# Four products of 32 tokens in place of two of 64 for the values of an mLSTM cell

## The chip, the cores and the metric

The kernel runs on one core of a Trainium2 chip. The metric is the time of one execution on the device in microseconds; several runs are made and their median is given. TensorE multiplies matrices, VectorE and ScalarE work element by element, GpSimd (POOL) does masks and small products, and SyncE (SP) issues the transfers.

## The reference

The computation has two parts. The first is an mLSTM cell over 4 batches, 8 heads, 768 tokens and a head width of 40, all in float32. Per head, with gates that are made stable by a running maximum `m`:

```
C = f * C + i * outer(v_t, k_t)        n = f * n + i * k_t
y_t = sigmoid(o_t) * (C q_t) / max(|n . q_t|, 1)
```

The second takes the cell's output as 3072 rows of 320 and computes `gelu(x @ w_in) @ w_out`, with the exact GELU and 2048 hidden columns.

## The kernel before

**Chunks.** The 768 tokens are cut into 6 chunks of 128 (numbered 0 to 5), so the recurrence becomes attention inside a chunk plus a state that is carried from chunk to chunk. For a batch `b` of a chunk, the steps of class `Cell` are:

- `weights` (ScalarE, L432): the decay matrix `W` of each head, 128 keys by 128 tokens;
- `scores` or `scores_two` (TensorE L507 or L523): keys times queries, which VectorE then multiplies into `W` (L510 or L529);
- `carry` (chunks 0 and 1: L545, L550) or `read_two` and `update_two` (later chunks: L578, L589): what the state gives to the queries, and the products of keys and weighted values that go into the state;
- `values` (L621): for each head, the weighted scores times the 128 values with a column of ones, that is 41 columns; VectorE adds what came from the state (L629);
- `finish` (L634 to L645): normalisation and output gate; `turn_y` (L656): the result is transposed into the layout of `x`; `split_x` (L674, L675).

Then `up` (L816, L827) computes the hidden columns with GELU on ScalarE (L831), and `down_steps` (L891) the second product, by sums and differences of blocks that VectorE prepares (`hidden_sums`, L748 to L750, `sum_late`, L921) and adds up (L904). The first chunk has its own steps for this (L761, L767, L868), because the weights are still being converted from their 64-bit form on VectorE and ScalarE (L357 to L374) then.

**Order.** Every engine works through its own queue in program order. That order is written out by hand as a string of letters in which each letter is a step and the digit its batch. `FRONT` plays chunks 0 and 1 and the first chunk's products; `DOWN` is played in each of the later rounds and interleaves the products `F` of one chunk with the cell of the next. Lower-case steps in `FRONT` are chunk 0, upper-case ones chunk 1; `V` is `values`. The parts of the two strings around it are:

```
FRONT: ... U U K L7 V0 K T2 r ... S2 J K W3 K V1 C2 ... J Y2 C3 X0 K V3 J K F ...
DOWN:  ... S0 K2 C0 F h0 M2 G0 G1 G2 G3 V0 V1 W2 F Q2 K3 Q3 Y0 M3 D3 F F N W3 F S2 F C2 h2 V2 V3 j F ...
```

In `DOWN`, `h0` and `h2` are `update_two` (L589), so TensorE goes from L589 straight to L621, as the letters between them are not TensorE's. In the last chunk `update_two` issues no products.

**Values in TensorE.** `Pm` holds 128 keys on the partitions and, per head, 128 tokens. A product's stationary operand is a slice `Pm[:, h, r]` of the tokens, its moving operand the head's 41 value columns, and its output goes to the partitions `r` of a PSUM tile `ph`. With `r` in `halves`, the slices have 64 tokens, and each product uses 64 of the array's 128 columns. From chunk 2 on the even heads come first, because VectorE weights them first.

Of the kernel before, what the change touches and what calls it, by code (L numbers as in the profile page):

```python
# [39 lines left out]
def kernel(  # L40
# [29 lines left out]
    R = P // 2  # L70
# [57 lines left out]
        return ob[n % NLD].rearrange("p (h d) -> p h d", d=D)  # L128

    halves = (slice(0, R), slice(R, P))  # L130

    def swapped(c, b):

        return c > 1 and b % 2 == 1
# [27 lines left out]
    def turn_of(n):  # L162

        return n % NLD if n < 2 * B else (n - 2 * B) % NQ

    def load_M(n, to=None):

        if not B <= n < NCH * B:
            return
        c, b = divmod(n, B)  # L170
        src = M_d[c - 1, b * H:(b + 1) * H, :]
        if to is not None:
            Mb[n] = to
            nc.sync.dma_start(out=to, in_=src.unsqueeze(0).to_broadcast([P, H, L]))
            return
        Mb[n] = shared([P, H, L], F32, "W") if n // 2 == NW else wts.tile([P, H, L], F32, name="W", tag="W")
        nc.sync.dma_start(out=Mb[n].rearrange("p h l -> p (h l)"),
                      in_=src.rearrange("h l -> (h l)").unsqueeze(0).to_broadcast([P, H * L]))
# [205 lines left out]
    def unread(bank):  # L384
        for _ in range(idle[0]):
            nc.tensor.matmul(bank, ident, ident, start=True, stop=True, skip_group_check=True)
        idle[0] = 0
# [4 lines left out]
    class Cell:  # L392
# [219 lines left out]
        def values(self, b):  # L612
            n = self.c * B + b
            Pm = W.pop(n)

            pool, tag = (ps_mm, "a") if self.c > 1 else (ps_h, "h")
            ph = pool.tile([P, H, D1], F32, name="ph", tag=tag)
            unread(ph.rearrange("p h d -> p (h d)")[:, 0:P])
            for h in range(H) if self.c < 2 else (*range(0, H, 2), *range(1, H, 2)):
                for r in halves:  # L620
                    nc.tensor.matmul(ph[r, h, :], Pm[:, h, r], vb[turn_of(n)][:, h, :], start=True, stop=True)  # L621
            if self.c > 1 and b > 0:
                load_M(n + NW)
            self.read(b)
            if self.c == 0:
                self.hs[b] = ph
                return
            hs = self.hs[b] = self.far.pop(b)
            nc.vector.tensor_tensor(out=hs, in0=ph, in1=hs, op=OP.add)  # L629
# [384 lines left out]
```

## Time and profile before

| | |
|---|---|
| Median of 3 runs | 480.7 us (480.67 to 480.8) |
| Span of the profiled execution, first to last instruction | 479.0 us |
| Median of the runs less that span (start and end around the instructions) | 1.7 us |
| TensorE busy | 470.5 us, 98% |
| VectorE, ScalarE, GpSimd busy | 351.5, 222.2, 70.4 us |
| Granted TensorE clock | 1.000 |
| Records of L621 | 768 matmuls, 768 weight loads |

The profiled execution's own time is the span and what lies around it; the runs' times stand within 0.13 us of each other, and 480.7 is taken for it. In the groups of instructions a line gives line, engine, operation, tiles, patch of the array in rows*columns, shape and number of records, then busy microseconds, mean nanoseconds of one record, and idle time before them with what ended it. PE is TensorE's matmul, PEld its weight load, DVE VectorE, ACT ScalarE. In a timeline or a chain a line begins with the start and the length in microseconds. Records of matmuls overlap, so the distance from start to start tells the pace and not the length of one.

### The profile page before, as it was taken

Reading aid. Unit: us, or ns where it says so; the run is one execution under the profiler, and the core shown is the slowest. Engines: PE = TensorE matmul, PEld = TensorE weight load, DVE = VectorE, ACT = ScalarE, POOL = GpSimd, SP = SyncE. Lnnn points to the kernel's source line nnn. Section 1 sums busy time; section 2 is a strip of 40 time slices with the busy share of each in tenths; the row PEclk is TensorE's granted clock in tenths of the full one; section 3 lists DMA queues with packets and bytes.
Section 4 is the critical chain, followed back from the end, with each engine's and each line's share of the span. In section 5 each row is a group of like instructions: output and inputs, shape, how many; then the busy total and the mean of one; then the engine's idle time right before and its main releaser. Section 6 shows DMA issues by size and latency. Waiting matters only on the chain.

```text
span 479.0 us, 11954 instructions
## 1 busy us (share of the span) xinstructions
PE 470.5 (98%) x4740; PEld 410.1 (86%) x4740; DVE 351.5 (73%) x762; ACT 222.2 (46%) x477; POOL 70.4 (15%) x104
## 2 busy tenths in 40 slices
PE   7899999999999999999999999999999999999997
PEld 7787888877777999977999977999977999977997
DVE  7899789798879999847589846589756599624321
ACT  6986999944532942112952113952113952112300
POOL 3001210000020225200324200324100222000000
PEclk9999999999999999999999999999999999999999
DMA  9998966289420367541356551367641350100001
GB/s 171 197 210 191 192 175 152 64 203 194 139 30 4 38 109 181 79 98 12 40 114 154 80 111 14 39 109 172 102 79 12 42 89 3 55 1 0 1 1 55
DMA packets 170423, 44.49 MB, mean 93 GB/s; under 512 B 156448, under 2 KB 163904, under 8 KB 170368
## 3 DMA queue, kind: packets, MB, share of 16 engines
q1 hardware_dynamic: 170368, 43.73, 46.4%
q8 instruction: 37, 0.61, 0.5%
q14 instruction: 18, 0.15, 0.1%
HBM read 39.58 MB, written 4.13 MB: 91 GB/s over the span
## 4 chain that ended last, share of the span: by engine, by line
PE 78%; issue 10%; DVE 7%; SPq 2%; DMA 1%; ACT 1%; POOL 0%; DVEq 0%; POOLq 0%
PE po L891 27%; PE pu L816 19%; PE po L868 7%; PE pu L761 5%; PE pu L827 5%; PE ph L621 4%; PE ps L523 2%; PE pu L767 1%; PE pf L589 1%; SPq L147 1%; PE px L656 1%; PE pf L578 1%; PE ps L507 1%; SPq L157 1%; PE pt L481 1%
## 5 line engine op out<-in xcount | busy, mean ns | idle before, releaser
L891 PE MATMUL po<-w_out,g 128*128 128x160 f32 x640 | 91.6, 301 | 0.0
L891 PEld LDWEIGHTS po<-w_out,g 128*128 128x128 f32 x640 | 87.7, 190 | 2.0 <-ACT g L831 1.8
L831 ACT ACTIVATE g<-pu 128x512 f32<-128x512 f32 x80 | 40.8, 614 | 52.9 <-PE pu L827 52.8
L891 PE MATMUL po<-w_sums,sums 128*128 128x160 f32 x320 | 47.7, 303 | 0.0
L891 PEld LDWEIGHTS po<-w_sums,sums 128*128 128x128 f32 x320 | 44.1, 190 | 0.7
L816 PE MATMUL pu<-x_hi,w_in_hi 128*128 128x512 f32 x160 | 41.7, 402 | 0.0
L666 ACT ACTIVATE x_hi<-px 128x384 fp32r<-128x384 f32 x20 | 9.8, 489 | 67.0 <-PE px L656 67.0
L816 PE MATMUL pu<-x_lo,w_in_lo 128*128 128x512 f32 x160 | 40.6, 395 | 0.0
L432 ACT ACTIVATE W<-W,aT 128x128 f32<-128x128 f32 x128 | 39.2, 388 | 0.1
L816 PEld LDWEIGHTS pu<-x_hi,w_in_hi 128*128 128x128 f32 x160 | 28.5, 188 | 9.3 <-ACT g L831 4.1
L748 DVE TENSOR_TENSOR sums<-g 128x512 f32<-128x512 f32 x20 | 13.8, 688 | 30.8 <-ACT g L831 30.8
L816 PEld LDWEIGHTS pu<-x_lo,w_in_lo 128*128 128x128 f32 x160 | 30.1, 188 | 7.2
L868 PE MATMUL po<-w_out,g 128*128 128x320 f32 x128 | 35.2, 433 | 0.0
L868 PEld LDWEIGHTS po<-w_out,g 128*128 128x128 f32 x128 | 24.0, 190 | 9.5
L831 ACT ACT_TABLE_LOAD x5 | 6.4, 1283 | 55.1 <-DMA blocks<-in_k_dram 27.6
L720 DVE TENSOR_TENSOR w_in_mid<-w_in_hi,w_in_lo 128x512 fp32r<-128x512 f32 x20 | 13.8, 688 | 24.4 <-PE pu L816 24.4
L816 PE MATMUL pu<-x_all,w_mid 128*128 128x512 f32 x80 | 31.6, 395 | 0.0
L816 PE MATMUL pu<-x_all,w_in_mid 128*128 128x512 f32 x80 | 31.6, 395 | 0.0
L444 POOL MEMSET g<- 32x1024 f32 x8 | 7.6, 945 | 150.1 <-ACT W L432 124.5
L406 POOL TENSOR_SCALAR_AFFINE_SELECT W<-W 128x1024 f32<-128x1024 f32 (+2 forms) x20 | 21.3, 1076 | 54.8 <-DMA W<-M_d 42.2
L904 DVE TENSOR_TENSOR o_sb<-po,o_sb 128x320 f32<-128x320 f32 (+1 forms) x27 | 12.5, 464 | 22.8 <-PE po L891 18.8
L761 PE MATMUL pu<-first_x,w_in 128*128 128x256 f32 x128 | 29.1, 382 | 0.1
(183 smaller groups left out, 915.6 us busy)
## 6 DMA issues: line engine op xcount, KB each, us to landing
W<-M_d SPq DMA_DIRECT2D x16, 512.0 KB, 5.6
bits<-in_moe_w_in_dram SPq DMA_DIRECT2D x20, 256.0 KB, 4.6
bits<-in_moe_w_out_dram SPq DMA_DIRECT2D x16, 320.0 KB, 3.3
ob<-in_o_gate_dram SPq DMA_DIRECT2D x24, 160.0 KB, 3.5
out_dram<-o_sb SPq DMA_DIRECT2D x24, 160.0 KB, 2.1
vb<-in_v_dram SPq DMA_DIRECT2D x14, 160.0 KB, 5.1
kb<-in_k_dram SPq DMA_DIRECT2D x14, 160.0 KB, 5.1
g<-M_d SPq DMA_DIRECT2D x4, 512.0 KB, 4.4
```

Of the source, the lines that this page charges most:

```text
L406: nc.gpsimd.affine_select(out=x, in_=x, compare_op=OP.is_ge, fill=1.0e30, base=base, pattern=[[0, H], [1, x.shape[2]]], channel_multiplier=-1)
L432: nc.scalar.activation(out=W[n][:, h, :], in_=src, func=AF.Exp, scale=-1.0, bias=aT[:, self.c, r:r + 1])
L621: nc.tensor.matmul(ph[r, h, :], Pm[:, h, r], vb[turn_of(n)][:, h, :], start=True, stop=True)
L720: nc.vector.tensor_tensor(out=w_mid[i], in0=w_hi[i], in1=w_lo[i], op=OP.add)
L748: nc.vector.tensor_tensor(out=s1, in0=a21, in1=a22, op=OP.add)
L761: nc.tensor.matmul(banks[-1][e][:, i - i0, :], in_tile(i, x)[:, e, i % 2 * P:(i % 2 + 1) * P], first_x[:, x, t0:t1], start=(x == 0 and i = ...
L816: nc.tensor.matmul(pus[i][e], w[k][:, e, i * P:(i + 1) * P], x[:, k, :], start=(n == 0 and k == 0), stop=False, skip_group_check=True)
L827: nc.tensor.matmul(pu[e], w[r, i // 2, i % 2 * P:(i % 2 + 1) * P], x[r, NX, :], start=False, stop=(n == 2), skip_group_check=True)
L831: nc.scalar.activation(out=g.t[:, HF * e + i, :], in_=pu[e], func=AF.Gelu, scale=4097.0)
L868: nc.tensor.matmul(po[b], g.t[:, f, b * L:(b + 1) * L], w_out[:, f, :], start=(f == 0), stop=(f == NF - 1))
L891: nc.tensor.matmul(bank[at][:, i, :], lhs(j, t), rhs(j), start=(first and i == 0 and j == 0), stop=(i == n - 1 and j == HF - 1), skip_grou ...
L904: nc.vector.tensor_tensor(out=to, in0=pb, in1=x, op=OP.add)
```

## The change

From the second chunk on (`self.c` of 1 and more), `values` loops over four slices of 32 tokens in place of two of 64. A head gets four products, each with a stationary operand of 128 by 32, the same 41 moving columns and an output of 32 partitions. The PSUM tile, the order of the heads and of all steps, and what is waited for stay. Chunk 0 keeps the halves.

```diff
     halves = (slice(0, R), slice(R, P))
+    quarters = tuple(slice(R // 2 * n, R // 2 * (n + 1)) for n in range(4))
...
             for h in range(H) if self.c < 2 else (*range(0, H, 2), *range(1, H, 2)):
-                for r in halves:
+                for r in halves if self.c == 0 else quarters:
                     nc.tensor.matmul(ph[r, h, :], Pm[:, h, r], vb[turn_of(n)][:, h, :], start=True, stop=True)
```

## The prediction

> **What bounds the kernel now.** I read the page first: the busy shares in 40 slices, then its chain that ended last.
>
> ```profile
> span 479.0 us, 11954 instructions
> ...
> PE   7899999999999999999999999999999999999997
> ...
> PE 78%; issue 10%; DVE 7%; SPq 2%; DMA 1%; ACT 1%; POOL 0%; DVEq 0%; POOLq 0%
> ```
>
> TensorE is busy from end to end and carries the chain, so an edit of TensorE's own stream moves the end directly, unless another engine is waiting just behind it. Second, the chain through the middle of chunk 2's cell, where each piece is TensorE:
>
> ```profile
> 162.38 1.50 PE ps L523 x64
> 163.88 0.91 PE pf L578 x64
> 164.79 2.37 PE po L891 x16
> 167.16 1.06 PE pf L589 x32
> 168.22 1.87 PE ph L621 x64
> ```
>
> L621 is the changed line. Two batches' values are 32 products; a product leaves two weight-load records and two matmul records, hence 64, in 1.87 us: 0.935 us for a batch, 29 ns a record. L578 makes the same 64 records with the same 41 moving columns in 0.91 us, 14 ns a record. Third, the groups by shape, to see why:
>
> ```profile
> L621 PE MATMUL ph<-vb,W 128*64 128x41 f32 x576 | 19.6, 231 | 0.4 <-DVE W L510 0.3
> L578 PE MATMUL pf<-state,qT 64*64 64x41 f32 x512 | 8.9, 227 | 0.0
> L621 PEld LDWEIGHTS ph<-vb,W 128*64 128x64 f32 x576 | 18.0, 138 | 1.6 <-DVE W L510 0.7 <-issue 0.5
> L891 PEld LDWEIGHTS po<-w_out,g 128*128 128x128 f32 x640 | 87.7, 190 | 2.0 <-ACT g L831 1.8
> ```
>
> The third word is the patch of the array, rows*columns. L621 uses 64 of 128 columns, so two records, one per half, share the array; L578 uses quarters of it and four share. So both walk in groups, 58 ns a pair in L621 (0.935/16), 57 ns a four in L578 (0.91/16).
>
> **What a group costs.** Streaming: a full-array record of 160 columns comes every 139 ns ((4.61-0.30)/31 in the timeline below), 0.87 ns a column; 41 columns take 35 ns. L621's 58 ns is therefore not streaming. Loading: the load of 128 columns lasts 190 ns and that of 64 lasts 138, so 52 ns for 64 columns, 0.81 ns each. 52 ns plus some 6 ns of handing over is the 58 ns: L621 waits for its weights. A quarter loads 32 columns: 26+6 = 32 ns, now below the 35 ns of streaming. With some 3 ns of handing over, as on the wide records (139 against 136 if I take 0.85 a column), I take 38 ns a group of four, if four column strips run at once. The batch keeps 16 groups (8 heads, two records deep): 16*38 = 0.61 us in place of 0.935, **0.325 us less**. There are 5 chunks*4 batches = 20: -6.5 us.
>
> No row shows four strips of 32 columns on all 128 rows. Bounds: 32 ns if loading alone counted, 58 ns if a four goes no faster than L578's fours, which is the row nearest in count, 76 ns if only two strips run together, which is as many as any row of 128 rows shows. I take 38 because both known causes of a longer group (load width, streamed columns) are there priced by rows; the ends stay for the range. Each ns of the group is 320*1 ns = 0.32 us.
>
> A rule that speaks against it: the Trainium skill, "TensorE: Matmul & The Clock Gate", section "Wait — 56ns, not 53.3ns?", holds that the starts of matmuls are never nearer than about 25 ns. L578's 14 ns a record contradicts it where records go to different parts of the array. By that rule a batch would be 64*25 = 1.6 us and the kernel some 14 us slower. The same page, "Measured speedup vs the span model", gives 2.38 times for three strips of 32 columns; as an estimate that makes the group 38*3/2.38 = 48 ns and the saving about half. No run here shows either.
>
> **Changes of shape.** Today L621 often follows or precedes lines on the same 128*64 patches; with 32 columns these become changes. The price, from two timelines:
>
> ```profile
> 157.76 4.61 PE L891 MATMUL po<-w_out,g 128*128 128x160 f32 x32
> ...
> 167.09 1.13 PE L589 MATMUL pf<-vw,kb 128*64 128x41 f32 x32
> 168.05 2.04 PE L621 MATMUL ph<-vb,W 128*64 128x41 f32 x64
> ```
>
> ```profile
> 398.35 1.14 PE L578 MATMUL pf<-state,qT 64*64 64x41 f32 x64
> 399.43 1.13 PE L621 MATMUL ph<-vb,W 128*64 128x41 f32 x32
> ```
>
> Same shape: L589 ends at 168.22, L621's first record at 168.05+0.23 = 168.28, 0.06 later. Other shape: L578 ends at 399.49, L621's first record at 399.43+0.25 = 399.68, 0.19 later. A change costs 0.13 us. New ones: L589 to L621 twice in each of chunks 2, 3, 4; L621 to L545 after V1 and V2 of chunk 1. The last chunk has no L589. So 8*0.13 = +1.0 us. The narrower first load could give 0.03 back at each; I leave it out.
>
> **What is late next.** The new products carry the same waits; none is added, and no DMA or queue moves. But TensorE now arrives earlier at things that it does not drive. In the cell the scores are weighted on VectorE (L529) just ahead of V3, and VectorE is held there by transposes of blocks that come by DMA.
>
> ```profile
> 400.91 0.44 DVE g L529
> 401.34 0.04 issue
> 401.39 0.67 PE ph L621 x16
> ```
>
> In the last chunk V3's odd heads already wait for the last L529. Only their own half is saved (0.16 us), plus what VectorE itself may come forward, 0.1: 0.3 in place of 1.3. In chunks 2 to 4 a cell brings V3's odd heads forward by 3.5 batches of 0.325, less two changes: 0.88 us. The slack is read as in chunk 3:
>
> ```profile
> 256.19 1.76 DVE L529 TENSOR_TENSOR g<-ps,g 128x256 f32<-128x256 f32 x4
> ...
> 257.91 1.11 PE L621 MATMUL ph<-vb,g 128*64 128x41 f32 x32
> ```
>
> L529 ends at 257.95; the odd heads begin half a batch after 257.91, at 258.38: 0.43 us. In chunks 2 and 4 it is 0.83 (185.38 against 186.21, 329.71 against 330.54). VectorE's own idle time before L904 (0.8 in chunk 3) lets it follow by perhaps 0.1 before its DMA holds it. So some 0.35 goes in chunk 3, about nothing in 2 and 4. In chunk 1, ScalarE is full (9.5 us busy of 10 from 60 to 70) and its copy of qT ends at 69.12, with L507 beginning at 69.32: of V0's 0.325 about 0.15 is lost.
>
> The sum: chunk 1, 4*0.325-2*0.13-0.15 = 0.9; chunks 2 to 4, 3*1.04-0.35 = 2.8; chunk 5, 0.3. Together **-4.0 us**. The profiled span is 479.0, the median of the runs 480.7, so 1.7 lies around the span and stays: 475.0 for the span, **476.7** in all. With all of the cover holding it is -6.5+1.0 = -5.5, 475.2; at a group of 45 ns, 478.5 or so.
>
> **Rivals.** (1) *Slower: the four strips do not run at once.* Place: each group of L621. They read the same 128 partitions in four streams, where the trace shows at most two (L621 itself, L550). With two at a time a four takes 76 ns: 320*(76-58.4) = +5.6, with the changes +1.0: 487.3. One at a time would be 320*(152-58.4) = +30. Break-even is where 320 groups give back just the 1.0 us of changes: 55 ns. Against it: L578 runs four at once, and its four 64-row patches are also two strips wide. (2) *The group stays at 58 ns*, because what paces L578's fours is the issue of eight instructions, not its 64-column loads: 480.7+1.0 = 481.7. L578 can't tell these apart, both give 57 ns; for it speaks that the products double, against it that starts inside such a four are far closer than 58/4. (3) *The gain is eaten by VectorE and ScalarE* further back (y, the turns of x, the next M): each of chunks 2 to 4 then keeps only V3's half, 0.16, and chunk 1 half its 0.9: -0.5-0.45-0.3 = -1.3, 479.4. Against it, the turns of x come after a dozen microseconds of products with slack of about 1 us at the last one. (4) That the change does nothing can be excluded: 320 more products must be issued.
>
> **How the numbers follow.** A measurement here can tell 0.2% (1.0 us) from no change. The forecast with its own range 475.2 to 479.0 has 0.56; a still shorter group 0.04, faster; rival 3, 479 to 480, 0.08, of which 0.06 faster and 0.02 the same; rival 2, just at the border, 0.12, of which 0.08 same and 0.04 slower; rival 1 0.20, slower. Faster 0.66, same 0.10, slower 0.24. The range takes in all but rival 1: 475.0 to 482.5.
>
> **What would show it.** The L621 rows should read 128*32 with 128x32 loads of about 138-26 = 112 ns and twice the count (1280 records from chunk 1 on, beside 128 old ones). The chain's piece for two batches should shrink from 1.87 to about 1.22 us; 1.87 would be rival 2, 2.4 rival 1. Weight loads before V0 of chunks 2 to 4 should show a new idle 0.17 from "issue". A wait of L621 for L529 in chunk 3 and a longer one in the last chunk would show where gain goes; if waits for VectorE stand before L656 or L816 too, it is rival 3. The prediction is wrong if the group is not near 38 ns, or if shape changes cost more than 0.2.

## The result and the profile after

The changed kernel takes **485.5 us** (median of 7 runs, 482.9 to 489.5), the kernel before 480.7 beside it (7 runs): a ratio of 1.0089, 95% interval 1.0067 to 1.0112. It is slower by 0.9%, where 0.8% faster was forecast, and the time lies above the forecast's range. The profiled execution took 489.5, the longest of the seven. Ratios here and below leave out runs more than 1.5% above the fastest of their kernel (two each in e9 and e15); the medians have all runs. From the page of after, span, busy shares, clock, the instruction queue and the shares of the chain:

```profile
span 487.5 us, 13234 instructions
...
PE   8999999999999999999999999989999999999997
...
PEclk9699999999999999999999999989999999999999
...
q8 instruction: 42, 0.69, 0.6%
...
PE 70%; issue 13%; DVE 9%; POOL 2%; ACT 2%; SPq 2%; DMA 1%; DVEq 0%; POOLq 0%; ACTq 0%
```

There are 1280 instructions more: 320 products more, each of two loads and two matmuls. The queue that brings instructions carried 42 packets, 37 before; 0.69 MB in 42 packets is 16.4 KB each, and 1280 instructions for 5 packets is 256 instructions in each. TensorE has a gap at two thirds of the span, and its clock two dips, one of them there. The dip in the second slice (half clock from 15 to 25 us, some 4 us lost) lies in chunk 0, whose code is the same in both kernels; runs of the kernel before beside the later experiments show dips too (485.2 us at a mean clock of 0.989), so I don't count it to the change. Next the groups of the changed line by shape:

```profile
L622 PE MATMUL ph<-vb,W 128*32 128x41 f32 x960 | 12.5, 202 | 0.3
L622 PEld LDWEIGHTS ph<-vb,W 128*32 128x32 f32 x960 | 10.7, 109 | 1.9 <-issue 0.9
L622 PE MATMUL ph<-vb,g 128*32 128x41 f32 x256 | 3.9, 203 | 2.2 <-DVE g L530 1.1 <-issue 1.0
```

and the waits of TensorE's matmuls (engine, line, what it waited for: microseconds in all, times, longest):

```profile
PE po L892 <- issue: 1.9, 2, 1.6
PE ph L622 <- issue: 1.5, 2, 1.0
...
PE ph L622 <- DVE g L530: 1.1, 4, 0.4
```

The loads last 109 ns, forecast 112. What is new is idle time that ends by "issue": by nothing that another engine did. A second profile of the same kernel (experiment e5_again, 485.1 us) has the chain of waits run through TensorE here; this is chunk 3's second pair of batches:

```profile
258.48 1.06 PE pf L590 x32
259.55 0.77 PE ph L622 x64
260.31 0.03 issue
260.34 0.38 PE ph L622 x15
260.72 0.99 issue
261.71 0.65 PE ph L622 x46
```

Before, two batches were one piece of 1.87 us. Now the first batch takes 0.77 us, but in the second one, between pieces of 0.38 and 0.65 us, TensorE stops for 0.99 us, though no operand is missing.

**Where it stops.** I numbered all TensorE records from the program's start, counting from 0 (loads, matmuls, semaphore instructions). The first records behind the stops at 97.5, 175.7, 190.1, 264.5 and 322.2 us of the first profile (the one at 190.1 is only 0.07 us long there) are numbers 2241, 3521, 4033, 6081 and 7361. The distances are 1280, 512, 2048 and 1280: all multiples of 256. In the second profile the stops stand at the same five numbers, with 0.47, 0.60, 0.62, 0.99 and 1.81 us. So TensorE stops where a block of 256 instructions ends. In the first profile packets of the instruction queue landed at 96.10, 174.24, 188.64, 263.11 and 320.65 us, 1.4 to 1.6 us ahead of the five restarts. Each of these packets was asked for 0.6 to 1.3 us after TensorE had entered the block before and took 0.9 to 1.5 us. From entering that block to entering the next one it was 3.3 to 3.9 us; I reckoned with 4.0.

The Trainium skill has a sentence on this that the forecast passed over: "Runtime: NRT & Kernel Launch", section "Terms", says that an engine's instruction memory is refilled in blocks of 16 KiB. The packets above agree.

The longest stop has a price of its own. Busy time and granted clock (the column PEclk) around it, first profile:

```profile
core 0: us, PE busy (x) PEld busy (x) DVE busy (x) ACT busy (x) POOL busy (x), PEclk, DMA share, GB/s
318.00:320.20 2.20, 2.15 (x152) 1.97 (x148) 2.12 (x5) 2.17 (x6) 0.74 (x1) 1.00 0.38 39
320.20:322.20 2.00, 0.43 (x12) 0.19 (x1) 2.00 (x8) 1.99 (x6) 0.26 (x1) 1.00 0.19 24
322.20:325.70 3.50, 3.48 (x13) 3.49 (x14) 0.01 (x1) 1.25 (x5) 0.54 (x1) 0.52 0.51 101
```

Two microseconds with little to do, then 3.4 us at half clock, which costs 1.7 us.

**Theory.** TensorE's instructions come in blocks of 256, one ahead, some 4.0 us each: 15.6 ns an instruction. Halves need 4 instructions in 58 ns (14.5 ns each), with L891's 74 ns each around them. Quarters need 8 in 39 ns (4.9 ns each), so a pair of batches uses up a block in 1.25 us. I replayed the first profile's TensorE records with blocks that are usable 4.0 us after the one before was entered. By this reckoning, which no view shows and which proves too kind below, there are stops of 4.0 us in all at four of the five places, and none in the kernel before. **Rival 1:** waits for VectorE and ScalarE. **Rival 2:** the clock. **Rival 3:** the strips themselves.

### The profile page after: what moved, and what is told of

The parts are those of the page before. It is cut to its first block, busy times and chain, and to the rows that moved or that the text cites. A ratio compares the mean times of both kernels' runs of the same rounds, so it can differ in the third digit from the quotient of the medians.

```text
span 487.5 us, 13234 instructions
## 1 busy us (share of the span) xinstructions
PE 474.4 (97%) x5380; PEld 411.0 (84%) x5380; DVE 351.2 (72%) x762; ACT 222.7 (46%) x477; POOL 72.0 (15%) x104
## 4 chain that ended last, share of the span: by engine, by line
PE 70%; issue 13%; DVE 9%; POOL 2%; ACT 2%; SPq 2%; DMA 1%; DVEq 0%; POOLq 0%; ACTq 0%
PE po L892 23%; PE pu L817 16%; PE po L869 7%; PE pu L762 5%; PE pu L828 4%; PE ph L622 3%; PE ps L508 2%; SPq L158 1%; PE pu L768 1%; PE px L657 1%; PE ps L524 1%; PE pt L482 1%; POOL g L407 1%; DMA g<-M_d 1%; PE pf L590 1%
## 5 line engine op out<-in xcount | busy, mean ns | idle before, releaser
L892 PE MATMUL po<-w_sums,sums 128*128 128x160 f32 x320 | 49.9, 310 | 1.9 <-issue 1.9
L892 PEld LDWEIGHTS po<-w_sums,sums 128*128 128x128 f32 x320 | 45.9, 196 | 3.1 <-issue 2.4
```

The lines of the kernel that those rows point to most:

```text
L892: nc.tensor.matmul(bank[at][:, i, :], lhs(j, t), rhs(j), start=(first and i == 0 and j == 0), stop=(i == n - 1 and j == HF - 1), skip_grou ...
```

## Experiments

| run | what | median us | ratio to before, 95% | idle at block ends in its profile, us |
|---|---|---|---|---|
| e5 | changed kernel again | 484.7 | 1.0066 (1.0050 to 1.0082) | 4.5 |
| e2 | changed, 32 instructions fewer at the start | 483.5 | 1.0056 (1.0034 to 1.0079) | 3.2 |
| e3 | changed, 32 more at the start | 491.1 | 1.0208 (1.0175 to 1.0241) | 8.7 |
| e4 | quarters for odd batches | 481.3 | 0.9998 (0.9979 to 1.0017) | 1.6 |
| e6 | changed, F ahead of each pair | 481.4 | 1.0008 (0.9991 to 1.0026) | 1.5 |
| e7 | e6 and e2 together | 480.4 | 0.9983 (0.9970 to 0.9996) | 0.2 |
| e8 | halves, F ahead of each pair | 482.5 | 1.0028 (1.0017 to 1.0039) | 0 |
| e9 | e7, second batch's first products ahead | 484.8 | 1.0065 (1.0033 to 1.0097) | 5.0 |
| e10 | e2, F from before the update | 488.3 | 1.0116 (1.0085 to 1.0147) | 2.4 |
| e11 | e10 and e9 together | 488.4 | 1.0130 (1.0104 to 1.0156) | 2.2 |
| e12 | e8, second batch's first products ahead | 483.0 | 1.0032 (1.0020 to 1.0044) | 0 |
| e13 | halves, padded | 516.9 | 1.0740 (1.0695 to 1.0784) | 0 |
| e14 | quarters, padded | 514.5 | 1.0676 (1.0638 to 1.0715) | 0.3 |
| e15 | e14, first products ahead | 518.0 | 1.0719 (1.0655 to 1.0783) | 0.7 |
| e16 | e2, F within each pair | 480.2 | 0.9976 (0.9952 to 1.0001) | 0.8 |
| e17 | changed, F within each pair | 480.4 | 0.9994 (0.9976 to 1.0011) | 1.7 |
| e18 | e17, halves in chunk 1 | 480.4 | 0.9982 (0.9969 to 0.9996) | 0.9 |

The kernel before had medians of 480.7 to 481.2 beside these. The last column sums the idle times over 0.2 us whose end is the beginning of a block.

### The supply by itself: e1_streams

```diff
+    for n in range(192):
+        for r in halves:
+            nc.tensor.matmul(cold[r, n % H, :], ident[:, r], w_out[:, 1, 0:D1], start=True, stop=True, ...)
...
+    for n in range(96):
+        for r in quarters:
+            nc.tensor.matmul(cold[r, n % H, :], ident[:, r], w_out[:, 1, 0:D1], start=True, stop=True, ...)
```

> The kernel before, with four streams of TensorE work appended behind its last product, each into a bank that nobody reads: 32 full products of 320 columns, 192 pairs of halves (128 rows x 64 columns, 41 moving), 32 full products again, 96 fours of quarters (128 x 32, 41 moving). Both middle streams are 384 products, 1536 instructions, six blocks of 256. Theory (TensorE's instructions come in blocks of 256, one block ahead, some 4.0 us from entering a block to the next one's being usable): both middle streams end up at the pace of the blocks, about 4.0 us for 256 instructions, 62 ns a product, some 24 us each; the quarters start their first block at 39 ns a four, then stand idle about 2.7 us at each block's end. Rival (the four strips themselves are slow in the kernel, or waits and the clock did it): no idle inside either stream, halves 58 ns a product (22 us), quarters 58/3 = 19.5 ns a product (7.5 us).

The timeline of TensorE's matmuls in the quarters' stream:

```profile
532.39 1.82 PE L996 MATMUL cold<-w_out,ident 128*32 128x41 f32 x173
536.11 1.40 PE L996 MATMUL cold<-w_out,ident 128*32 128x41 f32 x128 [1.90 <-issue]
539.57 1.99 PE L996 MATMUL cold<-w_out,ident 128*32 128x41 f32 x128 [2.06 <-issue]
543.57 2.41 PE L996 MATMUL cold<-w_out,ident 128*32 128x41 f32 x128 [2.02 <-issue]
547.02 1.40 PE L996 MATMUL cold<-w_out,ident 128*32 128x41 f32 x128 [1.04 <-issue]
550.75 1.72 PE L996 MATMUL cold<-w_out,ident 128*32 128x41 f32 x83 [2.33 <-issue]
```

and the halves (L991) beside them in the groups:

```profile
L991 PE MATMUL cold<-w_out,ident 128*64 128x41 f32 x768 | 22.6, 230 | 0.0
...
L996 PE MATMUL cold<-w_out,ident 128*32 128x41 f32 x768 | 10.7, 227 | 9.3 <-issue 9.3
```

Each burst is 128 matmuls and as many loads, 256 instructions in 1.4 us (2.0 to 2.4 at half clock), and then TensorE waits for 1.0 to 2.3 us. From start to start the blocks take 3.45 to 4.00 us, 3.66 in the mean: 14.3 ns an instruction, a little better than the 15.6 expected. The halves run without a stop at 22.4 us for 384 products, 58 ns each or 14.6 ns an instruction; the expectation of 62 ns for them was wrong, they are just slow enough. The quarters need 20.3 us for as many, where 96 groups of 39 ns would be 3.7: nearly all that the strips save is lost to the supply. Nothing else ran here, so rivals 1 and 3 are out as the cause of such stops. The mean clock over the quarters' stream was 0.77, over the halves' 1.00.

### The same work at another place in its block: e2_back32, e3_fwd32

```diff
-    warm(6)
+    warm_wide(3)
```

`warm_wide` has 256 moving columns where `warm` has 128; the edit is made at both places, and at two more `warm(2)` becomes `warm_wide(1)`.

> The changed kernel, and its warm-up products at the start of the program are made half as many and twice as wide (two times 6 of 128 columns become 3 of 256, two times 2 become 1): the same TensorE time, 8 products or 32 instructions fewer, so every later instruction stands 32 places earlier in its block of 256. Nothing else changes. Theory (instruction blocks): of the five stalls that make some 4 us, the replay leaves one, of about 1.4 us at the second pair of chunk 3; 482 to 483 us, about 2.5 to 3 us under the changed kernel's 485.5. Rival 1 (waits for VectorE and ScalarE) and rival 3 (the pace of the strips): no difference, 485 to 486. Rival 2 (clock): no difference beyond the scatter of the changed kernel, 482.9 to 489.5.

```diff
     warm(6)
+    cold = ps_h.tile([P, P], F32, name="cold", tag="h")
+    for r in 2 * quarters:
+        nc.tensor.matmul(cold[r, 0:32], w_out[:, 0, r], w_out[:, 0, 0:32], start=True, stop=True, ...)
```

> The changed kernel with 8 quarter products (0.3 us, 32 instructions) more in TensorE's idle before the turned gates, at the start: every later instruction stands 32 places later in its block of 256. Theory (instruction blocks): the stalls move to other places (172.8, 262.8, 319.6, 339, 410.7 in the changed kernel's time) and grow from 4.0 to about 7.1 us: 488 to 489 us, 3 us over the changed kernel. Rivals 1, 2 and 3: no difference but the 0.3 us at most: 485 to 486.

483.5 and 491.1, 0.5 and 2 us over what was expected, and 7.6 us apart, by 64 instructions of filler in the first 21 us of the program. In e3 the stops stand at 170.3, 190.7, 262.1, 320.0, 340.1 and 411.4 us; the replay had named all but the second. TensorE's waits in e3:

```profile
PE ph L625 <- issue: 7.8, 5, 2.1
...
PE po L895 <- issue: 0.9, 1, 0.9
```

In e2 the stop at 262 us is the forecast one (1.4 us); those at 187 (1.5) and 258 us (0.3) were not in the replay, which is too kind. The first records behind all these stops are again numbers that leave 193 when divided by 256, as those above do. Neither rival 1 nor rival 3 can move 7.6 us by filler. Nor can rival 2: the mean clock over the runs was 0.9937 in e3 and 0.9964 in e2, a difference of some 1.3 us in 485. That leaves the blocks.

### Fewer, later, in another order: e4_odd to e8_halves_moved

```diff
-                for r in halves if self.c == 0 else quarters:
+                for r in quarters if self.c > 0 and b % 2 else halves:
```

> The changed kernel with quarters for the odd batches alone (10 of 20); even batches keep halves, so a pair has 192 instructions in 1.55 us in place of 256 in 1.25. Theory (instruction blocks): the replay has no stall left. Each odd batch is 0.31 us shorter and pays 0.13 for its exit and, in the 8 pairs, 0.10 for the change from halves: -1.1 us in all, 479.3 to 480.7 us, not above the kernel before. Rival 1 (VectorE and ScalarE) and rival 3 (strips slow in the kernel): about half of the changed kernel's loss, 483 us. Rival 2 (clock): half or all of the loss, 482 to 485.

481.3, level with the kernel before on that chip (481.1) and 0.6 us over the expected range. Most of the loss is gone with half of the quarters, as the theory has it, but not all: 1.6 us of stops in L590, ahead of the values of two pairs, which the replay lacked.

> The changed kernel as it is, so that the other kernels of this row have it on the same chip. All theories: 483 to 487 us, median 485.5; the stalls for instructions at the same places as in the first profile (97, 175, 190, 264, 322 us), whatever the clock does.

Measured 484.7 (483.5 to 485.3), the five stops as told above.

```diff
-    ... C0 F h0 M2 G0 G1 G2 G3 V0 V1 W2 F Q2 ... C2 h2 V2 V3 j F Y1
+    ... C0 F h0 M2 G0 G1 G2 G3 F V0 V1 W2 Q2 ... C2 h2 F V2 V3 j Y1
```

> The changed kernel with one step of the written order moved: the product of the down projection that followed each pair of values (32 instructions in 2.4 us) now stands before the pair, eight times. Theory (instruction blocks): the 448 to 608 instructions that came in one run are cut by 2.4 us; the replay keeps 0.7 us of stall at chunk 1's last batch (its order is another list, untouched) and some 0.4 elsewhere, of 4.0; the pairs' waits for VectorE go as well: 480 to 481.5 us, 4 to 5 under the changed kernel. Rival 1 (VectorE and ScalarE are what ate the gain): the move gives them 2.4 us more before each pair as well, but the profile shows only 1.1 us of such waits: 484 us, with the idle for instructions still there. Rival 2 (clock) and rival 3 (pace): no difference, 485.

> The same move, with the halved count of warm-up products of e2_back32 (every instruction 32 places earlier). Theory (instruction blocks): the replay has no stall anywhere; what is left is the gain of the quarters: 478 to 479.7 us, faster than the kernel before. Rivals 1, 2 and 3: as e6_moved.

> The kernel before (halves everywhere) with the same move of eight steps. It tells whether the move itself brings anything. Theory (instruction blocks): halves never ran out of instructions, so within 0.5 us of the kernel before. A rival to the theory's reading of e6_moved (the order itself is better, whatever the values): 1 us or more under the kernel before.

e6 came to 481.4 and e7 to 480.4: the stops are down to 1.5 and 0.2 us, and the time with them. e7 is 0.7 us over its expected range. e8 missed: the move costs halves 1.5 us. It puts a product of another shape between `h0` and `V0`, which had the same one: a change into it and one out of it. Counted in the traces, the patch changes from one matmul to the next 129 times in e8 and 116 times before; 13 at 0.13 us are 1.7 us, an estimate that covers the loss. e7 has 131. So in like order, and with almost no stops, quarters bring 482.5-480.4 = 2.2 us. The forecast 4.0 had charged them six changes in chunks 2 to 4, 0.8 us, which the halves pay here too: 2.2 is less than half of 4.8. The rest shows in the two timelines, chunk 2's first pair with halves (e8), then quarters (e7):

```profile
170.58 2.06 PE L621 MATMUL ph<-vb,W 128*64 128x41 f32 x64
172.58 1.63 PE L891 MATMUL po<-w_out,g 128*128 128x160 f32 x10
```

```profile
169.82 1.56 PE L628 MATMUL ph<-vb,W 128*32 128x41 f32 x128
171.31 1.90 PE L898 MATMUL po<-w_out,g 128*128 128x160 f32 x12
```

From the pair's start to the next product's it is 2.00 us, then 1.49; in six of e7's other pairs it is about 1.60, and longer by a stop in the seventh. Two batches at 0.62 with 0.13 at the end would be 1.37. The difference is a hole between the batches, 0.14 us here and 0.25 in the other pairs. In the trace's records two or three semaphore instructions stand there 0.11 us apart. With halves (the kernel before, 240 us) the same three are read from 240.59 to 240.81, while TensorE still has products until 241.10: they are hidden. With quarters (246 us of after) they are read at 246.28, 246.39 and 246.50, the last two after the first batch's last product has begun at 246.35, and the next load begins at 246.57.

### Hiding the semaphores: e9_ahead to e12_halves_ahead

`begin` takes a batch's PSUM tile and weights, and `some` issues the products of the heads that it is given:

```diff
...
+                part, self.next = begin(b), begin(b + 1)
+                some(part, heads[:1])
+                some(self.next, (0, 1))
+                some(part, heads[1:])
...
```

> e7_moved_back, and in each pair of chunk 2 and later the products of the second batch's first two heads are issued straight behind the first head of the first batch, so that the semaphore instructions that the second batch needs stand near the pair's beginning, behind a product of 2.4 us, and not in its middle. Theory (instruction supply, here its second part: three semaphore instructions of some 106 ns each that TensorE's queue no longer has a lead to hide): the 0.14 to 0.27 us in the middle of each of the 8 pairs goes, 1.3 to 1.7 us in all: 478.7 to 479.2 us. Rival (those gaps are the wait for VectorE's last product of the scores, L530, which has only moved): the wait moves to the pair's beginning and nothing is won, 480.4 us.

The hole is gone, and the time is worse, 484.8. First the same pair as above, then chunk 4's first pair, both of e9:

```profile
169.29 1.42 PE L631 MATMUL ph<-vb,W 128*32 128x41 f32 x128
170.65 2.58 PE L915 MATMUL po<-w_out,g 128*128 128x160 f32 x17
```

```profile
314.06 1.39 PE L631 MATMUL ph<-vb,W 128*32 128x41 f32 x124
317.53 0.27 PE L631 MATMUL ph<-vb,W 128*32 128x41 f32 x4 [2.08 <-issue]
```

The first pair takes 1.36 us in place of 1.49, and most others 1.36 in place of 1.60: the theory's gain. But TensorE now runs into a block's end three times, in a pair or soon behind one, for 2.1, 1.4 and 1.6 us. Expectation and replay were wrong on the total: what the pair saved, the supply took back with interest.

```diff
-    ... S0 K2 C0 F h0 M2 G0 G1 G2 G3 V0 V1 ... F S2 F C2 h2 V2 V3 ...
+    ... S0 K2 C0 h0 M2 G0 G1 G2 G3 F V0 V1 ... F S2 C2 h2 F V2 V3 ...
```

> e2_back32 (the changed kernel with 32 fewer warm-up instructions) with another move than e7_moved_back's: the product of the down projection in front of the pair comes from before the state's update (first pair) and from before its reading (second pair), not from behind the values. With quarters this costs no change of array shape, where e7_moved_back's costs one for a pair. Theory (instruction blocks): 192 to 320 instructions in one run stay ahead of the product, 256 behind it; the replay has no stall at 4.0 us a block and 0.9 us at 4.4; 8 shape changes at 0.1 to 0.13 us saved against e7_moved_back, 479.2 to 480.4 us. Rival (VectorE, which gets 2.4 us less between the reading and the values than in e7_moved_back, is what bounds the pair): its waits (L530) are back, 481 to 482.

> e10_order2 with the second batch's first products ahead, as in e9_ahead. Theory: both gains, 477.8 to 479 us, faster than the kernel before by 2 to 3 us. Rival (VectorE): the second batch's weights are wanted 0.6 us earlier, so the wait grows by as much as the gap that goes: as e10_order2.

Both missed by 8 and 9 us: 488.3 and 488.4. I had not asked who waits when the state's update comes 2.4 us earlier. The waits of e10:

```profile
PE pf L596 <- POOL vw L501: 3.5, 2, 2.1
PE pf L596 <- issue: 2.4, 1, 2.4
```

The update (L596) now waits for GpSimd's weighted values, and one block's end costs 2.4 us; behind both kinds of idle time of over 2 us the clock falls (0.68 in the mean of the 3.5 us after 183.1, 0.58 in the 3.5 us after 258.9). The rival, VectorE's L530, was not it either. So these two runs tell nothing of the blocks.

> e8_halves_moved (halves, the product in front of the pair) with the second batch's first products ahead. With halves the queue's lead of some 0.5 us hid the semaphore instructions, so the theory expects no change: 482.3 to 482.7 us. If this order helps for another reason it gains as much as e9_ahead does: 481.

483.0, 0.2 us over the expected range and not better than e8's 482.5: with halves there is no hole to close, as expected.

### With time to spare: e13_pad_halves to e15_pad_ahead

```diff
+            for _ in range(10 if self.c > 1 and b % 2 == 0 else 0):
+                nc.tensor.matmul(ph.rearrange("p h d -> p (h d)")[:, 0:2 * P], ident, ident.unsqueeze(1).to_broadcast([P, 2, P]), ...)
```

> The kernel before, with ten products of 256 columns (0.45 us each, 40 instructions) put in front of the first batch of each pair from chunk 2 on, into the bank that the batch writes next: 4.5 us of TensorE time with few instructions, eight times. The base for the next two. Both theories: 35 to 36 us more than the kernel before, 515 to 517 us.

> The changed kernel with the same ten products in front of each pair: instructions have time to come in, and so have VectorE and ScalarE. Theory (the quarters themselves do what was forecast; blocks of instructions and the semaphores in the middle of a pair took it back): 0.40 us less a pair than e13_pad_halves (a pair 1.87 to 1.50 us, entry and exit alike), 3.2 in all, and about 0.1 in chunk 1 with its stall: 3 to 4 us under e13_pad_halves. Rival (the gain is given back wherever the next engine is late, with or without stalls): 1 us under it or less.

> e14_pad_quarters with the second batch's first products behind the first head of the first batch, as in e9_ahead. Theory: the 0.24 us in the middle of each pair goes, 1.9 us in all, and the padding keeps instructions coming, unlike e9_ahead: 5 to 6 us under e13_pad_halves, which is near the forecast's 5.5 of quarters and shape changes alone. Rival (what e9_ahead saved in the pairs comes back by itself as another wait, block or no block): as e14_pad_quarters.

516.9 and 514.5; the spans of the two profiles, both at full clock, are 514.9 and 511.6, 3.3 us apart, where 3 to 4 was expected. The medians are 2.4 apart, less than expected. Chunk 4's first pair, e13 and then e14:

```profile
335.32 2.07 PE L624 MATMUL ph<-vb,W 128*64 128x41 f32 x64
337.31 2.44 PE L894 MATMUL po<-w_sums,sums 128*128 128x160 f32 x16
```

```profile
333.62 1.67 PE L625 MATMUL ph<-vb,W 128*32 128x41 f32 x128
335.21 2.44 PE L895 MATMUL po<-w_sums,sums 128*128 128x160 f32 x16
```

1.99 and 1.59 us from start to next start: 0.40 a pair, 3.2 for the eight. That is what quarters are worth in these pairs where instructions don't run out, with the hole between the batches still in. e15's times spread from 513.8 to 530.2 at clocks of 0.981 to 1.000 and decide nothing. In its profile the distance from chunk 1's first to the last pair's start is 369.8 us, 370.3 in e14 and 373.3 in e13, with a stop of 0.7 us in e15; I leave it as inconclusive.

### Cutting the run in two: e16_mid, e17_mid_plain, e18_mid_late

```diff
-    ... V0 V1 W2 F Q2 ... h2 V2 V3 j F Y1
+    ... V0 F V1 W2 Q2 ... h2 V2 F V3 j Y1
```

> e2_back32 with the down product that followed each pair moved between the two batches of the pair instead of in front: 128 instructions of quarters, 32 in 2.4 us, 128 of quarters. The semaphores of the second batch stand behind a long product, and the longest run of dense instructions is cut in two; one more change of shape for a pair than e7_moved_back (0.10 to 0.15 us). Theory: 1.7 us won and 0.8 to 1.2 lost against e7_moved_back, no stall in the replay: 479 to 480 us, 1 to 2 under the kernel before. Rival (the run of 608 instructions over the cell counts, not the burst within a pair): stalls of 3 to 5 us as in e9_ahead, 483 to 485.

> The changed kernel with the down product between the two batches of each pair, as in e16_mid, and the warm-up products as they were (no shift by 32 instructions). Theory (instruction blocks): cut in two, the runs hardly depend on where the blocks end, but chunk 1's stall of 0.7 us (its order is untouched) is back, and the replay has up to 1.1 us more at 4.4 us a block: 480.5 to 482 us, 0.5 to 1.5 over e16_mid. Rival (the shift did nothing, e16_mid's gain is all of the order): as e16_mid, 480.2.

> e17_mid_plain with halves in chunk 1, quarters from chunk 2 on. Its four batches have 64 instructions fewer each, 256 in all, so every later instruction keeps its place in its block and the later chunks are those of e17_mid_plain. Theory: chunk 1's four batches lose 0.28 us of pace and win 0.1 us of shape changes each, 0.7 us in all, and the stall of 0.5 to 0.7 us there goes: as e17_mid_plain within 0.5 us. Rival (quarters in chunk 1 are free of the supply limit): 0.7 us over it.

480.2, 480.4 and 480.4, the first 0.2 us over what was expected, the second 0.1 under. Chunk 4's first pair in e16, with the long product between the batches:

```profile
312.88 0.81 PE L628 MATMUL ph<-vb,W 128*32 128x41 f32 x64
313.62 2.44 PE L898 MATMUL po<-w_sums,sums 128*128 128x160 f32 x16
315.99 0.81 PE L628 MATMUL ph<-vb,W 128*32 128x41 f32 x64
316.73 1.49 PE L898 MATMUL po<-w_out,g 128*128 128x160 f32 x9
```

Each batch takes 0.74 us and there is no hole. One stop of over 0.5 us is left from chunk 2 on, in its second pair (0.8 us in e16, 0.9 in e17, 0.6 in e18); e17 has one of 0.6 in chunk 1 besides. e17 differs from e16 by 0.2 us, so once the run is cut it matters little where the blocks end; chunk 1 gains as much by quarters as it loses (e17 and e18). No version beats the kernel before by more than 0.3%; e7 and e18 have intervals just below 1, e16's ends at 1.0001.

## Why the prediction was wrong

- **The pace of a group** held. Undisturbed batches of chunk 1 have their 64 records in 0.62 us, 39 ns a four, forecast 38; loads of 109 ns, forecast 112. The strips run four at once, so rival 1 of the prediction (76 ns) is out, and so is rival 2, that a group stays at 58 ns. Starts 10 ns apart in the mean also go below the 25 ns floor that the Trainium skill's page "TensorE: Matmul & The Clock Gate", section "Wait — 56ns, not 53.3ns?", states for the starts of matmuls. 39 ns is also better than the 48 estimated from that page's 2.38 times (section "Measured speedup vs the span model").
- **Changes of shape** held: L622 to L546 costs 0.18 us from end to end, 0.05 before; L590 to L622 0.15, 0.05 before. That is 0.13 and 0.10, forecast 0.13.
- **Waits for VectorE** held in size, not in place: 1.1 us at L530, four times, in chunks 2 and 5 (forecast 0.35 in chunk 3 and 1.0 of the last chunk's gain).
- **The step that failed** is the sentence "The new products carry the same waits; none is added, and no DMA or queue moves." It is true of the products, but it put the supply of the 1280 instructions more, and what had been hidden behind the slower groups, at nothing. TensorE runs out of instructions at block ends: 4.5 us in the second profile, 8.7 in e3, 0.2 in e7, for the same products. And the semaphore instructions between the batches of a pair, which were there before and hidden, make a hole of 0.14 to 0.25 us in each of 8 pairs where 0.04 is the usual distance, some 1.6 us. From the first to the last start, two batches take 1.81 us before, 1.47 with the hole and 1.23 in e9, where it is closed; the forecast piece was 1.22.
- **The rivals** missed it too. Rival 2 named "the issue of eight instructions", but as the pace of a single group, where a burst of 256 runs at full pace. Its limit is an average over some 4 us, which no row of a single line shows.

The sum by measured terms: -6.2 for 20 batches at 0.31, +0.9 and -0.3 for shapes and narrower first loads, +1.6 for the holes, +0.5 to 1.1 for VectorE, +4.5 for the idle time of the stops: +1.0 to 1.6 us. But a stop costs more than its idle time. The products of chunk 4 around the longest stop, in the second profile and in the kernel before:

```profile
317.40 0.40 PE L892 MATMUL po<-w_sums,sums 128*128 128x160 f32 x1
319.62 2.31 PE L892 MATMUL po<-w_sums,sums 128*128 128x160 f32 x15 [1.81 <-issue]
...
328.37 1.57 PE L524 MATMUL ps<-qT,kT 64*64 64x128 f32 x64
```

```profile
314.35 2.44 PE L891 MATMUL po<-w_sums,sums 128*128 128x160 f32 x16
...
323.25 1.57 PE L523 MATMUL ps<-qT,kT 64*64 64x128 f32 x64
```

10.97 us against 8.90 for the same work: 2.07 more, with 1.81 of idle time and the clock at 1.00. Around the stop of 0.60 us it is 0.88 more, and in the first profile 0.62 around the one of 0.34. With 0.27 more for each of five stops (an estimate from these three) the sum is +2.3 to 2.9. In the second profile TensorE lags 1.36 us at chunk 1's first values (64.17 against 62.81; the clock was 0.91 over the first 20 us) and 4.15 at the end: 2.8 us lost from there on, as the sum has it. The runs of the changed kernel at full clock were 2.2 to 4.8 us over the kernel before; half clock behind a stop comes on top in others (1.7 us at the one above). Why the stops differ from run to run stays open, as only profiled executions show them.

## What to carry to other kernels

A product cut into more and smaller ones must be paid in instructions too: count the instructions that TensorE needs over any 4 us, and compare them with the 256 that came in 3.3 to 4.0 us here. The neighbours count, not the line alone: four strips came out level to 0.2% ahead where a long product with few instructions stood beside each batch, and lost where three dense steps followed one another. When a time moves by microseconds because a few instructions were added far away, look at the numbers of the instructions behind the idle time, for a common remainder by 256.

## What the runs showed of the hardware

- Instructions came by DMA in packets of 16 KB, 256 instructions, and a sustained stream of quarters ran at 3.66 us a block (14.3 ns an instruction), with stops; halves, at 3.73 us a block, ran without. TensorE went on 1.2 to 1.6 us after the packet had landed, and a stop cost 0.26 to 0.28 us more than its idle time.
- A semaphore instruction by itself took 0.11 us of TensorE's sequencer; with 58 ns groups it was hidden, with 39 ns groups it was not.
- Half clock stood behind some stops of 2 us (after: 0.52 over 3.5 us), and not behind others (e9's 2.1 us, clock 1.00). What decides it was not tried.
